# Summing over the head dimension: accumulating DMAs in place of indicator matmuls, with weight loads in 1 KB rows by contraction half

## The chip, the cores and the metric

The kernel runs on one core of one Trainium2 chip. The metric is the device time of one execution in microseconds (us); lower is better. A "span" is the profiled execution as the trace shows it; it is 1.5 to 2 us shorter than the time that is measured around it. Engines are called PE (matmuls), DVE (vector), ACT (activation), POOL (GpSimd, here it mainly issues DMAs) and SP (issues the loads).

## The reference

A gate mixes two branches over 2048 positions of width 512 (bfloat16):

```python
g = sigmoid((x * gate_w).sum(-1))               # one number a position
a = A(x)                                        # 32 heads of 16, each query sees 8 keys, 2 apart
b = B(x)                                        # layernorm, then an MLP over the POSITIONS
return g * a + (1 - g) * b

# A: logits[h, s, w] = sum_d q[h, s, d] * k[h, s - 2w, d] / 4 ; masked softmax over w (8) ; weighted sum of v ; @ wo
# B: u = gelu(h^T @ w1 + b1)  (2048 -> 1792) ; y = u @ w2 + b2  (1792 -> 2048) ; transposed back
```

The sum over `d` (16 head dimensions) is what this study is about. The layout splits the 16 dimensions 4 by 4: along one factor they lie in four tiles (`dl`), along the other in four neighbouring partitions. So DVE multiplies and adds over `dl`, and something must add partitions 4j, 4j+1, 4j+2 and 4j+3. The kernel's DVE operations all work within a partition and do not do that.

## The kernel before

The kernel is one list of operations with data dependences. A small planner in the file gives each a guessed duration, simulates the engines, and so fixes the order on every engine **before** the kernel runs. On the chip each engine works through its fixed order and waits at each operation for semaphores. An operation that is late holds everything behind it on its engine.

The parts that matter, with cuts:

```python
# the planner's guess of a DMA's end: one shared "DMA is free at" clock, 300 GB/s, 2 us of latency
def schedule(self, dma_bw=300e3, dma_lat=2.0, n_iter=3): ...
    xs = max(st + 0.3, dma_free); xd = max(op.nbytes / dma_bw, 0.05)
    dma_free = xs + xd
    op.end = max(dma_free, clock[e]) + dma_lat

# the sum over 4 neighbouring partitions: RP is a 0/1 matrix, 4 column groups at once, 16 matmuls a head half h
def f_sum(h, b0, with_gate): ...
    for wp in range(4):
        for c in range(4):
            ins = e.matmul(ps[32*c:32*c+32, 4+wp, :], lhsT=RP, rhs=sub(PB[b0], ...), tile_position=(0, 32*c))
A("pe", f_sum(h, b0, h == 0), ..., writes=LGB, name="sum%d" % h)
A("act", act(LOG[h], ps[:, 4:8, :], AF.Copy), 1.9, reads=LGB, writes=["log%d" % h], name="lev%d" % h)
# then on DVE: mask add, max tree (mx4, mx2, mx1), subtract (msub); on ACT exp; on DVE sum tree and normalisation (nrm)

# the normalised weights are copied to all partitions, a quarter of the positions each (four broadcasts, 512 KB each)
for c in range(4):
    prev = sch.dma("pool", ... dma_start(AVW[h] part c, ATT[h][32c:32c+32] repeated 4 times) ..., name="av%d_%d" % (h, c))

# weights times values for unit u (256 positions); for u = 3, 4, 5 half of the adds are an accumulating DMA
AV(tt(pv, V5..., AVW[h]..., ALU.mult), 4.4, ..., name="avm%d" % u)
if u in (3, 4, 5):
    sch.dma("pool", ... dma_start(pw(0, 4), pw(4, 4), accum_op=ALU.add) ..., name="avd%d" % u)
# later: avb (pair sum), avc -> ot[u], which PE's Wo matmuls of tiles 2u and 2u+1 need

def ld_w1(j):   # 7 loads of 1 MB, 256 columns each: rows of 512 bytes; ld_w2(j) likewise, 8 loads
    load("w1_%d" % j, W1H[j], w1v[:, :, 256*j:256*j+256], ...)
late_dep[0] = [qkd[0, 1]]   # w1_1, w1_2, wo, ... wait for the second accumulating DMA of the first q*k products
```

## Time and profile before

The kernel before takes 165.37 us (median of 3 runs, 165.23 to 165.86).

| What | Value | View |
|---|---|---|
| span, granted PE clock | 163.9 us, 1.0 | page, cores |
| PE in the chain of waits | 95% | page, part 4 |
| DVE busy | 92%, its waits on DMA 0.3 us | page, part 1; waits |
| attention's last sum on DVE ends | 158.7 us | timeline of DVE |

These are two lines of the page of the kernel before: busy time, share of the span and number of instructions of PE (part 1), and the lines of the chain that ended last (part 4).

```profile
PE 159.3 (97%) x793; PEld 77.5 (47%) x808; DVE 150.7 (92%) x126; ACT 70.2 (43%) x100; POOL 12.0 (7%) x36
...
PE ps L858 29%; PE ps L885 29%; PE ps L649 23%; PE ps L894 8%; PE ps L588 3%; DMA arena<-in_A_x_dram 2%; PE ps L722 1%; ACT arena L453 1%; PE ps L567 1%; PE ps L717 1%; DVE arena L579 0%; PE ps L604 0%
```

The chain is nearly all matmuls: L858 is the first MLP product, L885 the second, L649 the projections, L894 the Wo product. L722 with 1% is the indicator sum.

The waits view of the kernel before (who waited for whom: us in total, times, longest):

```profile
ACT arena L453 <- PE ps L894: 37.7, 11, 6.6
...
DVE arena L450 <- DMA arena<-arena: 0.3, 1, 0.3
```

ACT waits for PE a great deal, which costs nothing. DVE waits for a DMA once, 0.3 us.

The timeline of DVE before (start, length of the group, what, and in brackets the idle time ahead of it), and the last line of that of PE:

```profile
32.42 38.90 DVE L450 TENSOR_TENSOR arena<-arena 128x4096 bf16<-128x4096 bf16 x24
...
71.72 63.81 DVE L450 TENSOR_TENSOR arena<-arena 128x16 f32<-128x16 f32 x34
135.86 22.84 DVE L450 TENSOR_TENSOR arena<-arena 128x2048 bf16<-128x2048 bf16 x14 [0.33 <-DMA arena<-arena]
161.29 0.41 DVE L934 TENSOR_SCALAR arena<-ps,arena 128x128 bf16<-128x128 f32 x1 [2.59 <-PE ps L894]
```

```profile
155.90 5.35 PE L894 MATMUL ps<-arena 128*128 128x512 bf16 x28
```

DVE has no gap worth the name between 32 and 158.7 us (135.86 + 22.84), and PE's last Wo matmuls run to 161 us. The last two tiles of them (14 and 15) need DVE's last sum. So both engines are full, and DVE has about 1 us of slack.

How long POOL's DMAs take before, from issue to landing: first the two accumulating 1 MB DMAs of the products, then the eight broadcasts.

```profile
DMA to landing us min/median/max: 8.0/9.0/10.0
```

```profile
DMA to landing us min/median/max: 7.3/11.7/15.3
```

### The profile page before, as it was taken

The numbers are of one execution on the slowest core, as the hardware profiler recorded it, in microseconds if no ns is written. First come the engines' busy times: TensorE is split into PE (matmuls) and PEld (weight loads), VectorE is DVE, ScalarE is ACT, GpSimd is POOL, SyncE is SP. The second block draws the span as 40 slices with busy tenths as digits, with TensorE's granted clock in tenths as the row PEclk, the third lists the DMA queues.
The fourth block names the chain that finished last, engine by engine and source line by source line (L and its number), as shares of the span: only waits on it lengthen the run. The fifth ranks groups of instructions, "written<-read, shape, count | busy, mean of one in ns | idle before, by whom it ended". The sixth has DMA issues, their size and how long they took to land.

```text
span 163.9 us, 1989 instructions
## 1 busy us (share of the span) xinstructions
PE 159.3 (97%) x793; PEld 77.5 (47%) x808; DVE 150.7 (92%) x126; ACT 70.2 (43%) x100; POOL 12.0 (7%) x36
## 2 busy tenths in 40 slices
PE   7999999999999999999999999999999999999993
PEld 3755555555544444444444344444444444444641
DVE  0589989999999999999999999999999999999971
ACT  3357677766672379753111258111121111111164
POOL 3000021020000000004000000002200222000000
DMA  4999969909499094999998974990998799991014
GB/s 153 288 233 253 254 128 291 199 11 188 91 304 308 1 247 120 256 290 290 298 263 233 270 203 142 298 232 10 283 254 192 185 204 201 211 222 38 32 58 135
DMA packets 44684, 32.24 MB, mean 197 GB/s; under 512 B 7940, under 2 KB 42244, under 8 KB 44676
## 3 DMA queue, kind: packets, MB, share of 16 engines
q1 hardware_dynamic: 41444, 22.06, 51.9%
q0 software_dynamic: 2512, 9.44, 27.2%
q10 hardware_dynamic: 720, 0.62, 1.1%
q8 instruction: 6, 0.10, 0.2%
q14 instruction: 2, 0.02, 0.0%
HBM read 18.88 MB, written 2.10 MB: 128 GB/s over the span
## 4 chain that ended last, share of the span: by engine, by line
PE 95%; DMA 2%; ACT 1%; issue 1%; DVE 0%
PE ps L858 29%; PE ps L885 29%; PE ps L649 23%; PE ps L894 8%; PE ps L588 3%; DMA arena<-in_A_x_dram 2%; PE ps L722 1%; ACT arena L453 1%; PE ps L567 1%; PE ps L717 1%; DVE arena L579 0%; PE ps L604 0%
## 5 line engine op out<-in xcount | busy, mean ns | idle before, releaser
L450 DVE TENSOR_TENSOR arena<-arena 128x4096 bf16<-128x4096 bf16 (+8 forms) x79 | 132.0, 1718 | 1.9 <-ACT arena L453 0.6
L885 PE MATMUL ps<-arena 128*128 128x512 bf16 (+2 forms) x234 | 50.0, 366 | 0.2
L858 PE MATMUL ps<-arena 128*128 128x512 bf16 x218 | 48.5, 379 | 0.3
L453 ACT ACTIVATE arena<-ps,arena 128x512 bf16<-128x512 f32 (+1 forms) x30 | 21.8, 731 | 60.7 <-PE ps L894 37.7
L453 ACT ACTIVATE arena<-ps 128x512 bf16<-128x512 f32 (+3 forms) x53 | 32.9, 629 | 18.3 <-PE ps L649 10.9
L649 PE MATMUL ps<-arena 128*128 128x512 bf16 x173 | 38.0, 379 | 0.2
L885 PEld LDWEIGHTS ps<-arena 128*128 128x128 bf16 x238 | 22.8, 98 | 25.9
L858 PEld LDWEIGHTS ps<-arena 128*128 128x128 bf16 x224 | 21.7, 98 | 26.8 <-issue 0.8
L649 PEld LDWEIGHTS ps<-arena 128*128 128x128 bf16 x176 | 19.9, 113 | 18.0
L894 PE MATMUL ps<-arena 128*128 128x512 bf16 (+2 forms) x67 | 15.6, 366 | 0.1
L453 ACT ACTIVATE arena<-arena 128x16 f32<-128x16 f32 (+5 forms) x10 | 6.7, 678 | 9.7 <-DVE arena L450 9.7
L692 DVE BATCH_NORM_STATS2 arena<-arena 128x6 f32<-128x512 bf16 x16 | 9.9, 679 | 0.5 <-DMA arena<-in_A_x_dram 0.5
L954 ACT ACT_TABLE_LOAD x7 | 9.0, 1283 | 2.8 <-issue 2.7
L894 PEld LDWEIGHTS ps<-arena 128*128 128x128 bf16 x68 | 6.5, 98 | 7.3
L790 POOL DMA_DIRECT2D arena<-arena x8 | 4.3, 556 | 75.2 <-DVE arena L450 75.2
L706 DVE TENSOR_SCALAR arena<-arena 128x512 bf16<-128x512 bf16 x16 | 5.3, 406 | 0.0
L579 DVE COPY arena<-ps 128x256 bf16<-128x256 bf16 x4 | 1.1, 291 | 4.4 <-PE ps L567 4.2
L827 POOL DMA_DIRECT2D arena<-arena x3 | 3.6, 1209 | 17.7 <-DVE arena L450 17.7
L747 POOL DMA_DIRECT2D arena<-arena x2 | 2.5, 1268 | 31.5 <-DVE arena L692 21.5
L588 PE MATMUL ps<-arena 128*128 128x256 bf16 (+1 forms) x27 | 4.4, 313 | 0.2
L588 PEld LDWEIGHTS ps<-arena 128*128 128x128 bf16 x28 | 3.1, 119 | 1.1 <-DVE arena L579 0.4
L551 PE MATMUL ps<-const-bfloat16-1.0 128*128 128x512 bf16 (+1 forms) x9 | 2.7, 483 | 0.8 <-PEq L1004 0.8
(30 smaller groups left out, 14.4 us busy)
## 6 DMA issues: line engine op xcount, KB each, us to landing
arena<-in_B_w_dram SPq DMA_DIRECT2D x7, 1024.0 KB, 6.5
arena<-in_B_w_dram SPq DMA_DIRECT2D x8, 896.0 KB, 9.9
arena<-arena POOLq DMA_DIRECT2D x5, 1024.0 KB, 10.0
arena<-arena POOLq DMA_DIRECT2D x8, 512.0 KB, 11.7
out_dram<-arena SPq DMA_DIRECT2D x15, 128.0 KB, 2.3
arena<-in_A_x_dram SPq DMA_DIRECT2D x3, 512.0 KB, 4.7
arena<-in_A_wqkv_dram SPq DMA_DIRECT2D x2, 256.0 KB, 4.3
arena<-in_A_wqkv_dram SPq DMA_DIRECT2D x1, 512.0 KB, 6.5
```

The costliest lines, as they stand in the source:

```text
L450: return lambda e: e.tensor_tensor(out=o_, in0=a_, in1=b_, op=op_)
L453: return lambda e: e.activation(out=o_, in_=i_, func=f_, **kw)
L588: ins = e.matmul(ps[:, dl, c0:c1], lhsT=sub(WQKV, dt * 3 * D + dl, [(4, 128)]), rhs=XT[:, dt, c0:c1], start=(dt == 0 and hb == 0), stop=(d ...
L649: ins = e.matmul(ps[:, bank, :], lhsT=sub(WQKV, dt * 3 * D + tn * D + dl, [(4, 128)]), rhs=XT[:, dt, sb * 512:(sb + 1) * 512], start=(dt = ...
L692: A("dve", (lambda t_: lambda e: e.bn_stats(out=ST6[:, t_, :], in_=X[:, t_, :]))(t), 0.67, reads=["x%d" % t], writes=["st%d" % t], name="s ...
L706: A("dve", (lambda t_: lambda e: e.tensor_scalar(out=X[:, t_, :], in0=X[:, t_, :], scalar1=col(RSTD, t_), scalar2=col(NMR, t_), op0=ALU.mu ...
L790: prev = sch.dma("pool", (lambda d_, s_: lambda e: e.dma_start(d_, s_))(dst, src), 524288, sch.dsem("av%d_%d" % (h, c)), issue=1.0, reads= ...
L827: sch.dma("pool", (lambda o_, i_: lambda e: e.dma_start(o_, i_, accum_op=ALU.add, max_dma_last_dim=4096))(pw(0, 4), pw(4, 4)), 1800000, sc ...
L858: ins = e.matmul(ps[:, bank, :], lhsT=W1H[ft // 2][:, st, 128 * (ft % 2):128 * (ft % 2) + 128], rhs=X[:, st, :], start=(st == 0), stop=(st ...
L885: ins = e.matmul(ps[:, bank, 0:c1 - c0], lhsT=W2S[i // 2][:, ft, 128 * (i % 2):128 * (i % 2) + 128], rhs=UT[:, ft, c0:c1], start=(ft == 0) ...
L894: ins = e.matmul(ps[:, bank, 0:c1 - c0], lhsT=OT[:, i // 2, dl, 128 * (i % 2):128 * (i % 2) + 128], rhs=WO[:, dl, c0:c1], start=False, sto ...
L954: e.preload_act_table_set(want)
```

## The change

The intent is to take 32 matmuls off PE and two evictions off ACT: the four partitions are added by DMAs instead. The weight loads, all but the first of W1, get rows of 1 KB instead of 512 bytes: each load then holds half of the contraction for 512 columns, so four PSUM tiles stay open at a time. Eight of the sixteen layernorm applications move from DVE to ACT. DVE finishes the products of the first half-block before those of the second, and the gate's matmuls stand by themselves (both left out below). The diff, cut to its core:

```diff
-        dma_free = 0.0
+        dma_free = {"pool": 0.0, "hw": 0.0}          # the planner: POOL's DMAs and the loads no longer share a clock
...
+            src = w1v[:, 8*((j-1)%2):8*((j-1)%2)+8, 256+512*((j-1)//2):768+512*((j-1)//2)] if j else w1v[:, :, 0:256]
...
         for t in range(NST):
+            if t >= NST - 8:
+                A("act", act(X[:, t, :], X[:, t, :], AF.Identity, scale=col(RSTD, t), bias=col(NMR, t)), 0.6, ...)
+                continue
...
-            A("pe", f_sum(h, b0, h == 0), ...)
-            A("act", act(LOG[h], ps[:, 4:8, :], AF.Copy), 1.9, reads=LGB, ...)
+            for s_ in range(2):                       # s_: half of the head half, 512 positions
+                for k_ in range(2):                   # fa: partition 4j+k += partition 4j+k+2   (256 KB, accumulate)
+                    fold("fa%d_%d%d" % (h, s_, k_), ..., True, 550000, ...)
+            for s_ in range(2):
+                for k_ in range(2):                   # fb: logits = partition 4j (128 KB, copy)
+                    for c in (2*s_, 2*s_+1):          # fc: logits += partition 4j+1 (128 KB, accumulate)
+                        fold("%s%d_%d" % ("fb" if k_ == 0 else "fc", h, c), ..., k_ == 1, 100000*(1+k_), ...)
...
+        # MLP 1: ft 0, 1, then three groups of four tiles, first contraction half of all four, then the second
+        # MLP 2: the same, four tiles a group; a fixed order for the tail
```

Each of the four half-blocks thus has a chain of three DMA steps: fold (fa), copy (fb), accumulate (fc). POOL waits for the landing of one before it issues the next. The Trainium skill (DMA: Bandwidth & Descriptors, "Two DMAs through the same engine are not ordered") asks for just that: a DMA that reads what an earlier one wrote must wait for its semaphore. So three landings in a row are the price of this way of adding.

More of the change, by code (lines that the diff above doesn't have):

```diff
@@ L202, in _pass @@
                 clock[e] = st + op.dur
-                xs = max(st + 0.3, dma_free)
+                ring = "pool" if e == "pool" else "hw"
+                xs = max(st + 0.3, dma_free[ring])
                 xd = max(op.nbytes / dma_bw, 0.05)
-                dma_free = xs + xd
-                op.end = max(dma_free, clock[e]) + dma_lat
+                dma_free[ring] = xs + xd
+                op.end = max(dma_free[ring], clock[e]) + dma_lat
             else:
@@ L363, in bass_gated_mix__sliding_local_dilated__mixer_token_mlp__prompt_kernel @@
         W1N = NST * 256
-        W1H = [view(n_, BF16, [(256, NST), (1, 256)], extra=k_ * W1N)
-               for n_, k_ in (("W1", 0), ("W1", 1), ("W1", 2), ("XT", 0), ("XT", 1), ("W1", 0), ("W1", 1))]
+        W1H = [view(n_, BF16, [(512, NST // 2), (1, 512)] if j_ else [(256, NST), (1, 256)], extra=k_ * W1N)
+               for j_, (n_, k_) in enumerate((("W1", 0), ("W1", 1), ("W1", 2), ("XT", 0), ("XT", 1), ("W1", 0), ("W1", 1)))]
         W1R = ["w1s0", "w1s1", "w1s2", "w1x0", "w1x1", "w1s0", "w1s1"]
         def w2view(name, extra=0):
-            return view(name, BF16, [(256, NFT), (1, 256)], extra=extra)
+            return view(name, BF16, [(512, NFT // 2), (1, 512)], extra=extra)
         XTALL = ["xt0_%d_%d" % (t, k_) for t in range(4) for k_ in range(2)] + ["xt1", "xt2", "xt3"]
@@ L536, in ld_w1 @@
         def ld_w1(j):
-            w1ld[j] = load("w1_%d" % j, W1H[j], w1v[:, :, 256 * j:256 * j + 256], S * 256 * 2, [W1R[j]] + (XTALL if j in (3, 4) else []), order=j < 3,
+            src = w1v[:, 8 * ((j - 1) % 2):8 * ((j - 1) % 2) + 8, 256 + 512 * ((j - 1) // 2):768 + 512 * ((j - 1) // 2)] if j else w1v[:, :, 0:256]
+            w1ld[j] = load("w1_%d" % j, W1H[j], src, S * 256 * 2, [W1R[j]] + (XTALL if j in (3, 4) else []), order=j < 3,
                            after=[w1ld[j - 1]] if j > 3 else [])
         def ld_w2(j):
-            w1ld[7 + j] = load("w2_%d" % j, W2S[j], w2v[:, :, 256 * j:256 * j + 256], F * 256 * 2, ["w2_%d" % j] + W2ALIAS[j], order=False,
+            w1ld[7 + j] = load("w2_%d" % j, W2S[j], w2v[:, 7 * (j % 2):7 * (j % 2) + 7, 512 * (j // 2):512 * (j // 2) + 512], F * 256 * 2, ["w2_%d" % j] + W2ALIAS[j], order=False,
                                after=[w1ld[6 + j]])
@@ L705, in bass_gated_mix__sliding_local_dilated__mixer_token_mlp__prompt_kernel @@
         for t in range(NST):
+            if t >= NST - 8:
+                A("act", act(X[:, t, :], X[:, t, :], AF.Identity, scale=col(RSTD, t), bias=col(NMR, t)), 0.6,
+                  reads=["rstd", "nmr", "st%d" % t], writes=["x%d" % t], name="ln%d" % t, prio=10)
+                continue
             A("dve", (lambda t_: lambda e: e.tensor_scalar(out=X[:, t_, :], in0=X[:, t_, :], scalar1=col(RSTD, t_), scalar2=col(NMR, t_),
@@ L708, in bass_gated_mix__sliding_local_dilated__mixer_token_mlp__prompt_kernel, with f_gate @@
               reads=["rstd", "nmr", "st%d" % t], writes=["x%d" % t], name="ln%d" % t, prio=-10)
-        def f_sum(h, b0, with_gate):
-            def fn(e):
-                ins = None
-                if with_gate:
-                    for dt in range(4):
-                        for c in range(4):
-                            ins = e.matmul(ps[32 * c:32 * c + 32, 3, :], lhsT=GWREP[:, dt, :],
-                                           rhs=sub(XT, dt * S + c * UT_, [(HS, 2), (1, UT_)]),
-                                           start=(dt == 0), stop=(dt == 3), tile_position=(0, 32 * c))
-                for wp in range(4):
-                    for c in range(4):
-                        ins = e.matmul(ps[32 * c:32 * c + 32, 4 + wp, :], lhsT=RP, rhs=sub(PB[b0], (c // 2) * 4096 + 2 * wp * 512 + (c % 2) * UT_, [(512, 2), (1, UT_)]),
-                                       start=True, stop=True, tile_position=(0, 32 * c))
-                return ins
-            return fn
-        LGB = ["b4", "b5", "b6", "b7"]
+        def f_gate(e):
+            ins = None
+            for dt in range(4):
+                for c in range(4):
+                    ins = e.matmul(ps[32 * c:32 * c + 32, 3, :], lhsT=GWREP[:, dt, :],
+                                   rhs=sub(XT, dt * S + c * UT_, [(HS, 2), (1, UT_)]),
+                                   start=(dt == 0), stop=(dt == 3), tile_position=(0, 32 * c))
+            return ins
+        A("pe", f_gate, 1.0, reads=XTALL + ["gwrep"], writes=["b3"], name="gate", prio=-100)
+        A("act", act(E32, ps[:, 3, :], AF.Relu, scale=-1.0, bias=ZMAX), 0.6, reads=["b3"], writes=["e32"], name="zclip")
+        A("act", act(EB, E32, AF.Exp, scale=-1.0, bias=ZMAX), 0.6, reads=["e32"], writes=["eb"], name="zexp", table=LOGEXP)
         PLAN = {0: (0, 1, 2), 1: (1, 2, 0)}
@@ L735, in qk @@
                 sb = 2 * h + s_
-                A("dve", tt(sub(PB[b_], s_ * 4096, [(512, NW), (1, 512)]), sub(QH[h], dl * HS + s_ * 512, [(0, NW), (1, 512)]),
-                            sub(KH[h], dl * KR + PAD + s_ * 512, [(-2, NW), (1, 512)]), ALU.mult), 2.25,
+                A("dve", tt(sub(PB[b_], s_ * 4096, [(NW * UT_, 2), (UT_, NW), (1, UT_)]), sub(QH[h], dl * HS + s_ * 512, [(UT_, 2), (0, NW), (1, UT_)]),
+                            sub(KH[h], dl * KR + PAD + s_ * 512, [(UT_, 2), (-2, NW), (1, UT_)]), ALU.mult), 2.25,
                   reads=["q%d_%d" % (dl, sb), "k%d_%d" % (dl, sb)] + (["k%d_%d" % (dl, sb - 1)] if s_ else ["khalo" if h else "kpad"]),
-                  writes=[PS[b_][s_]], name="qk%d_%d_%d" % (h, dl, s_))
+                  writes=[PS[b_][s_]], name="qk%d_%d_%d" % (h, dl, s_), prio=-4 * (1 - s_))
             def qadd(x_, y_, s_, h=h):
                 A("dve", tt(sub(PB[x_], s_ * 4096, [(1, 4096)]), sub(PB[x_], s_ * 4096, [(1, 4096)]), sub(PB[y_], s_ * 4096, [(1, 4096)]), ALU.add), 2.25,
-                  reads=[PS[y_][s_]], writes=[PS[x_][s_]], name="qa%d_%d%d_%d" % (h, x_, y_, s_))
+                  reads=[PS[y_][s_]], writes=[PS[x_][s_]], name="qa%d_%d%d_%d" % (h, x_, y_, s_), prio=-4 * (1 - s_))
             def qaddd(x_, y_, s_, h=h):
@@ L755, in bass_gated_mix__sliding_local_dilated__mixer_token_mlp__prompt_kernel @@
                 qk(2, bb[2], s_)
-            for s_ in range(2):
                 qk(3, bb[1], s_)
                 qadd(bb[2], bb[1], s_)
-            for s_ in range(2):
                 qadd(bb[0], bb[2], s_)
             b0 = bb[0]
-            A("pe", f_sum(h, b0, h == 0), 1.2 + (1.0 if h == 0 else 0), reads=PS[b0] + ["rp"] + ((XTALL + ["gwrep"]) if h == 0 else []),
-              writes=LGB + (["b3"] if h == 0 else []), name="sum%d" % h, prio=-100, delay=0.2)
-            if h == 0:
-                A("act", act(E32, ps[:, 3, :], AF.Relu, scale=-1.0, bias=ZMAX), 0.6, reads=["b3"], writes=["e32"], name="zclip")
-                A("act", act(EB, E32, AF.Exp, scale=-1.0, bias=ZMAX), 0.6, reads=["e32"], writes=["eb"], name="zexp", table=LOGEXP)
@@ L767, in bass_gated_mix__sliding_local_dilated__mixer_token_mlp__prompt_kernel, with par, fold @@
-            A("act", act(LOG[h], ps[:, 4:8, :], AF.Copy), 1.9, reads=LGB, writes=["log%d" % h], name="lev%d" % h, prio=-30)
+            pst = PB[b0].ap[0][0]
+            def par(ap_, p0, dims, offs):
+                return bass.AP(ap_.tensor, ap_.offset + p0 * pst + offs, [list(d) for d in dims])
+            def fold(name, o_, i_, acc, nb, reads, writes):
+                kw = dict(accum_op=ALU.add, max_dma_last_dim=4096) if acc else {}
+                sch.dma("pool", lambda e: e.dma_start(o_, i_, **kw), nb, sch.dsem(name), issue=1.1, reads=reads, writes=writes, name=name)
@@ new lines, in bass_gated_mix__sliding_local_dilated__mixer_token_mlp__prompt_kernel @@
+            for s_ in range(2):
+                for k_ in range(2):
+                    fold("fa%d_%d%d" % (h, s_, k_), par(PB[b0], k_, [(4 * pst, 32), (1, 4096)], s_ * 4096), par(PB[b0], k_ + 2, [(4 * pst, 32), (1, 4096)], s_ * 4096),
+                         True, 550000, [PS[b0][s_]], ["fa%d_%d%d" % (h, s_, k_)])
+            for s_ in range(2):
+                for k_ in range(2):
+                    for c in (2 * s_, 2 * s_ + 1):
+                        fold("%s%d_%d" % ("fb" if k_ == 0 else "fc", h, c), psub(LOG[h], 32 * c, 32, 0, [(1, NW * UT_)]), par(PB[b0], k_, [(4 * pst, 32), (1, NW * UT_)], c * NW * UT_),
+                             k_ == 1, 100000 * (1 + k_), [PS[b0][s_], "fa%d_%d%d" % (h, s_, k_)], ["log%d_%d" % (h, c)])
@@ L768, in bass_gated_mix__sliding_local_dilated__mixer_token_mlp__prompt_kernel @@
+            LGR = ["log%d_%d" % (h, c) for c in range(4)]
             if h == 0:
                 A("dve", tt(psub(LOG[0], 0, 32, 0, [(UT_, NW), (1, PAD)]), psub(LOG[0], 0, 32, 0, [(UT_, NW), (1, PAD)]), MASK, ALU.add), 0.2,
-                  reads=["mask"], writes=["log0"], name="msk", prio=-30)
+                  reads=["mask"], writes=["log0", "log0_0"], name="msk", prio=-30)
             TR = ["s4", "s2", "s1"]
-            A("dve", tt(M4, LOG[h][:, 0:4, :], LOG[h][:, 4:8, :], ALU.max), 0.65, reads=["log%d" % h], writes=["s4"], name="mx4_%d" % h, prio=-30)
+            A("dve", tt(M4, LOG[h][:, 0:4, :], LOG[h][:, 4:8, :], ALU.max), 0.65, reads=["log%d" % h] + LGR, writes=["s4"], name="mx4_%d" % h, prio=-30)
@@ L773, in bass_gated_mix__sliding_local_dilated__mixer_token_mlp__prompt_kernel @@
             A("dve", tt(M2, M4[:, 0:2, :], M4[:, 2:4, :], ALU.max), 0.4, reads=["s4"], writes=["s2"], name="mx2_%d" % h, prio=-30)
             A("dve", tt(M1, M2[:, 0, :], M2[:, 1, :], ALU.max), 0.25, reads=["s2"], writes=["s1"], name="mx1_%d" % h, prio=-30)
-            A("dve", tt(LOG[h], LOG[h], sub(M1, 0, [(0, NW), (1, UT_)]), ALU.subtract), 1.2, reads=["s1"], writes=["log%d" % h], name="msub%d" % h, prio=-30)
+            A("dve", tt(LOG[h], LOG[h], sub(M1, 0, [(0, NW), (1, UT_)]), ALU.subtract), 1.2, reads=["s1"], writes=["log%d" % h] + LGR, name="msub%d" % h, prio=-30)
@@ L857, in fn @@
                 for st in range(8 * half, 8 * half + 8):
-                    ins = e.matmul(ps[:, bank, :], lhsT=W1H[ft // 2][:, st, 128 * (ft % 2):128 * (ft % 2) + 128], rhs=X[:, st, :],
-                                   start=(st == 0), stop=(st == NST - 1))
-                return ins
-            return fn
-        MLPB = [1, 2, 0, 1, 2, 0, 3, 1, 2, 0, 3, 1, 2, 0]
-        for ft in range(NFT):
-            bank = MLPB[ft]
-            for half in range(2):
-                PE(f_ph2(ft, bank, half), 1.735, ["x%d" % t for t in range(8 * half, 8 * half + 8)] + [W1R[ft // 2]], ["b%d" % bank],
-                   "ph2_%d_%d" % (ft, half))
-            A("act", act(UT[:, ft, :], ps[:, bank, :], AF.Gelu_apprx_tanh, bias=col(B1C, ft)), 0.7,
-              reads=["b%d" % bank, "b1c"], writes=["ut%d" % ft] + (["wq0", "wq1", "wq2", "wq3", "wk0", "wk1", "wv"] if ft == 0 else []), name="gel%d" % ft, table=GELU)
-            if ft % 2 == 1 and ft // 2 + 5 <= 6:
-                ld_w1(ft // 2 + 5)
+                    w_ = W1H[0][:, st, 128 * ft:128 * ft + 128] if ft < 2 else W1H[1 + 2 * ((ft - 2) // 4) + half][:, st % 8, 128 * ((ft - 2) % 4):128 * ((ft - 2) % 4) + 128]
@@ new lines, in fn, with mlp1 @@
+                    ins = e.matmul(ps[:, bank, :], lhsT=w_, rhs=X[:, st, :], start=(st == 0), stop=(st == NST - 1))
+                return ins
+            return fn
+        def mlp1(ft, half):
+            bank = (4 + ft) if ft < 2 else (ft - 2) % 8
+            j = 0 if ft < 2 else 1 + 2 * ((ft - 2) // 4) + half
+            PE(f_ph2(ft, bank, half), 1.735, ["x%d" % t for t in range(8 * half, 8 * half + 8)] + [W1R[j]], ["b%d" % bank], "ph2_%d_%d" % (ft, half))
+            if half:
+                A("act", act(UT[:, ft, :], ps[:, bank, :], AF.Gelu_apprx_tanh, bias=col(B1C, ft)), 0.7,
+                  reads=["b%d" % bank, "b1c"], writes=["ut%d" % ft] + (["wq0", "wq1", "wq2", "wq3", "wk0", "wk1", "wv"] if ft == 0 else []), name="gel%d" % ft, table=GELU)
@@ L873, in bass_gated_mix__sliding_local_dilated__mixer_token_mlp__prompt_kernel @@
+        for ft in range(2):
+            for half in range(2):
+                mlp1(ft, half)
+        ld_w1(5)
+        for g_ in range(3):
+            for half in range(2):
+                for ft in range(2 + 4 * g_, 6 + 4 * g_):
+                    mlp1(ft, half)
+                if (g_, half) == (0, 0):
+                    ld_w1(6)
         for j in range(8):
             ld_w2(j)
-        LAG = 5
-        ring[0], ring[1] = 0, [3, 4, 5, 6, 7, 1, 2, 0]
-        banks = {}
+        BK = {i: (4, 5, 6, 7, 0, 1, 2, 3)[i % 8] for i in range(NST)}
@@ L884, in fn @@
                 for ft in range(7 * half, 7 * half + 7):
-                    ins = e.matmul(ps[:, bank, 0:c1 - c0], lhsT=W2S[i // 2][:, ft, 128 * (i % 2):128 * (i % 2) + 128], rhs=UT[:, ft, c0:c1],
+                    ins = e.matmul(ps[:, bank, 0:c1 - c0], lhsT=W2S[2 * (i // 4) + half][:, ft % 7, 128 * (i % 4):128 * (i % 4) + 128], rhs=UT[:, ft, c0:c1],
                                    start=(ft == 0), stop=False)
@@ L902, in finish_tile @@
         def finish_tile(i):
-            bank = banks[i]
+            bank = BK[i]
             PE(f_wo(i, bank, 0, D), 0.87, ["ot%d" % (i // 2), "wo"], ["b%d" % bank], "wo%d" % i)
@@ L908, in finish_tile, with mlp2 @@
                     reads=["outs%d" % (i % 4)], name="d_out%d" % i)
+        TAILORDER = ([("m", 12, 0), ("m", 13, 0), ("w", 8), ("m", 14, 0), ("m", 15, 0, 0), ("w", 9), ("m", 15, 0, 1), ("m", 12, 1), ("m", 13, 1), ("m", 14, 1),
+                     ("m", 15, 1, 0), ("m", 15, 1, 1)] + [("w", i) for i in range(10, 15)])
         L = NST - 1
-        for i in range(L):
-            banks[i] = bank_()
-        head = ((0, 0), (1, 0), (2, 0), (0, 1), (1, 1), (2, 1))
-        for i, half in head + tuple((i, half) for i in range(3, L) for half in range(2)):
-            bank = banks[i]
-            PE(f_ph3(i, bank, half), 1.52, ["ut%d" % ft for ft in range(7 * half, 7 * half + 7)] + ["w2_%d" % (i // 2)], ["b%d" % bank], "ph3_%d_%d" % (i, half))
-            if half == 1 and i >= LAG:
-                finish_tile(i - LAG)
-        lastb = [bank_(), bank_()]
-        CH = ((0, 384), (384, 512))
-        for hf, (c0, c1) in enumerate(CH):
-            for half in range(2):
-                PE(f_ph3(L, lastb[hf], half, c0, c1), 0.77, ["ut%d" % ft for ft in range(7 * half, 7 * half + 7)] + ["w2_%d" % (L // 2)], ["b%d" % lastb[hf]],
-                   "ph3_%d_%d" % (L, half))
-        for i in range(L - LAG, L):
-            finish_tile(i)
+        CH = ((0, 384), (384, 512))
+        lastb = [BK[L], BK[8]]
+        def mlp2(i, half, hf=None):
+            bank = BK[i] if hf is None else lastb[hf]
+            c0, c1 = (0, D) if hf is None else CH[hf]
+            PE(f_ph3(i, bank, half, c0, c1), 1.52 * (c1 - c0) / D, ["ut%d" % ft for ft in range(7 * half, 7 * half + 7)] + ["w2_%d" % (2 * (i // 4) + half)], ["b%d" % bank],
+               "ph3_%d_%d%s" % (i, half, "" if hf is None else "ab"[hf]))
+        for b_ in range(3):
+            for half in range(2):
+                for i in range(4 * b_, 4 * b_ + 4):
+                    mlp2(i, half)
+                    if half and b_:
+                        finish_tile(i - 4)
+        for st_ in TAILORDER:
+            if st_[0] == "w":
+                finish_tile(st_[1])
+            else:
+                mlp2(*st_[1:])
         for hf, (c0, c1) in enumerate(CH):
```

## The prediction

> What bounds the kernel now. The chain of waits is PE for 95% of a 163.9 us span; the granted clock is 1.0 and no view shows PE waiting for weights or banks. But VectorE (DVE) is nearly co-critical. Its timeline has no gap over 0.5 us between 21.8 us and its last attention sum (ends 158.7 us), and the last five Wo groups on PE, of which the last two need that sum, run from 156.1 to 160.4 us. So PE has no idle time and DVE about 1 us of slack: a gain needs both to get shorter.
>
> What the change removes. PE: 32 indicator matmuls, 2 x about 0.9 us in the chain = 1.8 us (the gate's 1.0 us stays, only earlier). ACT: two evictions of the sums, 1.88 us each. DVE: 8 of 16 layernorm applications, 0.33 us start to start, 2.6 us; ACT takes them (about 0.6 us each) in a stretch where it is 70% busy, which the seven banks absorb. Without new waits both chains end 2 to 2.6 us earlier, about 163.
>
> What it adds. For each of four half-blocks a chain of three dependent DMAs from POOL: fold (accumulate), copy, accumulate; each waits for the landing of the one before. An uncontended accumulating DMA before (1 MB, issued at 35.0 us) had its first packet 1.8 us after issue start, moved 256 packets of 4 KB at about 0.35 us on 16 engines, and took 8.0 us. Estimate from that for the quarter-size fold: 3.5 to 4 us, then 2.5 and 3: about 10 us for a half alone. The Trainium skill (DMA: Bandwidth & Descriptors, "Issuing engines are not separate DMA queues") says that DMAs of all issuers share the same 16 engines. The trace agrees: with weight loads queued, POOL DMAs began 3.8, 5.0 and 3.2 us after issue, when the loads' backlog had nearly drained.
>
> The chains meet such backlogs. First half: folds issue near 41 us, just when W1 and Wo (2.6 MB, about 8 us) are released. Its result lands at 54 to 57 us, but DVE's fixed order wants it (mask add) near 52: 2 to 5 us stall. The last half issues near 95 to 98 us, beside three W2 loads: 0 to 4 us before the second max. 1 KB rows shorten loads a little (46 ns per 1 KB against 27 to 34 ns per 512 B) but loads were never waited for.
>
> Bigger: the second softmax is normalised later in DVE's order, directly before three multiplies (avm3 to avm5). Before, its end was followed by 22.5 us of DVE work until the first POOL-added sum was used, which landed 22 us after (four broadcasts of 9 to 15 us queue in front). Now only about 14 us of work lie between: up to 8 us stall, first at the multiply that needs the first broadcast (8.9 us to landing), then at that sum. PE's fixed order needs that sum for the seventh Wo group (tile 6), with 22 us of PE work behind it, so PE idles too.
>
> Sum: 165.4 - 2.3 (removed) + 2 to 5 (fold waits) + about 4 to 6 (broadcast and sum waits not hidden) is about 170.5 us; range 164.5 to 176. Faster over 2%: 0.04; within: 0.30; slower: 0.66.
>
> Right if: DVE's waits name DMA arena<-arena at the mask, the maxima, the multiplies and the pair sums, 5 to 12 us in total; PE shows a gap of 3 us or more before a Wo group (tile 6) at 135 to 147 us; DMA leaves PE's share of the chain below 92%.
>
> Wrong if: POOL packets interleave with loads instead of waiting for their backlog (folds land within 10 us, so 163 to 166); broadcasts without a weight load beside them land in 4 us; or PE waits for W1/W2 halves.

## The result, and the profile after

The changed kernel takes 200.83 us (median of 4 runs, 200.42 to 201.31) against 165.3 us before on the same chip. Executions over 1.5% slower than the fastest of the same kernel are left out of the means. The ratio is 1.2145 (95% interval 1.2103 to 1.2187). Ratios in this document are the mean time of one kernel's fast runs over that of the other's of the same rounds, so they are not quite the ratio of the quoted medians.

The page of the changed kernel: PE's busy line, the rows of DVE and of the granted clock in 40 slices (tenths), and the chain that ended last by engine and by line.

```profile
PE 167.7 (84%) x776; PEld 78.5 (39%) x776; DVE 148.8 (75%) x118; ACT 67.1 (34%) x104; POOL 31.0 (16%) x60
...
DVE  1689999999407960199992699999991950799970
...
PEclk9999999999999999999969999975759985589999
...
DMA 47%; DVE 30%; PE 14%; issue 4%; POOL 2%; ACT 1%; SPq 0%; DVEq 0%; POOLq 0%
DMA arena<-arena 45%; DVE arena L451 25%; PE ps L903 7%; PE ps L912 4%; DVE arena L694 4%; DMA arena<-in_A_x_dram 2%; POOL arena L768 2%; PE ps L590 1%; DVE arena L712 1%; ACT arena L454 1%; PE ps L651 1%; SPq L495 0%; PE ps L569 0%; DVE arena L684 0%; DVE arena L701 0%
```

PE's share of the chain has gone from 95% to 14%. "DMA arena<-arena", DMAs from on-chip memory to on-chip memory, takes 45% of it. The row of DVE has holes (4, 0, 6, 2, 1, 5), and after 99 us PE's clock falls to 5 tenths in some slices.

The waits view after:

```profile
POOL arena L768 <- DMA arena<-arena: 40.9, 8, 7.4
DVE arena L451 <- DMA arena<-arena: 37.0, 5, 10.6
...
PE ps L912 <- DVE arena L451: 20.0, 2, 13.7
...
PE ps L903 <- ACT arena L454: 7.7, 2, 4.3
```

DVE's five large waits on DMA are 37.0 us, against 0.3 before. The span grew by 35.2 us (199.1 - 163.9). DVE's busy time fell by 1.9 us (150.7 to 148.8). So nearly the whole loss passes through these five waits. POOL itself waits 40.9 us inside the chains (L768 is the fold) for one step to land before it may issue the next.

Where the five are, from the timeline of DVE after (bracket: idle time ahead of the group, and what ended it):

```profile
60.93 0.20 DVE L451 TENSOR_TENSOR arena<-arena 32x112 bf16<-32x112 bf16 x1 [9.15 <-DMA arena<-arena]
...
83.83 22.07 DVE L451 TENSOR_TENSOR arena<-arena 128x1024 bf16<-128x1024 bf16 x16 [10.65 <-DMA arena<-arena]
111.09 38.37 DVE L451 TENSOR_TENSOR arena<-arena 128x8192 bf16<-128x8192 bf16 x23 [5.19 <-DMA arena<-arena]
153.52 8.76 DVE L451 TENSOR_TENSOR arena<-arena 128x8192 bf16<-128x8192 bf16 x2 [4.06 <-DMA arena<-arena]
170.20 22.85 DVE L451 TENSOR_TENSOR arena<-arena 128x2048 bf16<-128x2048 bf16 x14 [7.92 <-DMA arena<-arena]
```

The first is the mask add (9.15 us, first half of head half 0), the second the first max (10.65 us, second half). The third is the first weighted multiply, waiting for its broadcast (5.19 us). The fourth and fifth are the multiply that needs the first broadcast of head half 1, and the first pair sum that reads what an accumulating DMA made (4.06 and 7.92 us).

The chains themselves, from the timeline of POOL after (each line a group of issues; bracket: what POOL waited for):

```profile
40.82 1.77 POOL L768 DMA_DIRECT2D arena<-arena  x2 [8.19 <-DVE arena L451]
48.89 1.14 POOL L768 DMA_DIRECT2D arena<-arena  x2 [6.30 <-DMA arena<-arena]
57.21 3.59 POOL L768 DMA_DIRECT2D arena<-arena  x4 [7.18 <-DMA arena<-arena]
68.25 1.14 POOL L768 DMA_DIRECT2D arena<-arena  x2 [7.45 <-DMA arena<-arena]
76.34 1.74 POOL L768 DMA_DIRECT2D arena<-arena  x2 [6.94 <-DMA arena<-arena]
...
118.01 1.83 POOL L768 DMA_DIRECT2D arena<-arena  x2 [12.90 <-DVE arena L451]
121.68 1.15 POOL L768 DMA_DIRECT2D arena<-arena  x2 [1.84 <-DMA arena<-arena]
124.95 1.75 POOL L768 DMA_DIRECT2D arena<-arena  x2 [2.12 <-DMA arena<-arena]
```

At 40.82 us the first folds are issued, at 48.89 the copies, at 57.21 the accumulates **and** the folds of the second half, at 68.25 and 76.34 us that half's copies and accumulates. The last chain, of head half 1, starts at 118.01 us: its steps follow each other after 3.7 and 3.3 us, not after 8. The record of landings gives the lengths from the first issue to the last landing that DVE waited for:

| Chain | Issued | Landed | Length | Weight loads beside it |
|---|---|---|---|---|
| head half 0, first half | 40.8 us | 60.8 (mask), 66.3 (all) | 20.0, 25.4 us | three at its start, four more later |
| head half 0, second half | 58.3 us | 83.7 us | 25.4 us | five |
| head half 1, first half | 89.1 us | 109.5 us | 20.4 us | four |
| head half 1, second half | 118.0 us | 129.3 us | 11.3 us | none |

The packets of POOL's queue show the difference at the start. In the last chain the first packet of the fold moves 1.47 us after issue. In the first chain it moves 5.18 us after, in the second chain the copies and the accumulates start after 4.00 and 4.36 us. In those microseconds the loads' queue moves 280 to 360 GB/s on average, and the new POOL DMA nothing. The third chain shows both cases side by side. Its two folds are issued at 89.07 and 89.66 us, a weight load at 90.20 us. The first fold lands after 3.68 us. The second moves its first packet 5.9 us after issue and lands after 9.02 us.

Landing times after, of the folds (L768), the broadcasts (L802) and the three pair-sum DMAs (L839):

```profile
DMA to landing us min/median/max: 2.7/7.4/10.3
```

```profile
DMA to landing us min/median/max: 8.7/12.6/17.9
```

```profile
DMA to landing us min/median/max: 17.0/17.8/20.4
```

The broadcasts were 7.3 to 15.3 us before; now 8.7 to 17.9. PE shows what becomes of it. This is its timeline around the largest gap:

```profile
155.95 1.03 PE L912 MATMUL ps<-arena 128*128 128x512 bf16 x4
156.82 1.67 PE L903 MATMUL ps<-arena 128*128 128x512 bf16 x7
172.21 1.89 PE L912 MATMUL ps<-arena 128*128 128x512 bf16 x4 [13.72 <-DVE arena L451]
```

L912 at 172.21 us is the Wo group of tile 6. It waits 13.72 us for DVE's pair sum, with about 22 us of PE work behind it in the fixed order. (The other L912 wait, 6.24 us, is that of tile 2.) Those four matmuls take 1.89 us where others take 1.03. The Trainium skill (TensorE: Matmul & The Clock Gate, "Part 1: The HAM clock gate") says that PE's clock drops to half after about 3.4 us of idling. The trace agrees: PE has nothing to do from 158.5 us on, and the granted clock, 1.00 from 159 to 162 us, is 0.50 from 163 to 172 us (windows view).

### The profile page after: what moved, and what is told of

Same layout as the page of the kernel before. It is cut to its first block, busy times and chain, and to the rows that moved or that the text cites. A ratio compares the mean times of both kernels' runs of the same rounds, so it can differ in the third digit from the quotient of the medians.

```text
span 199.1 us, 1964 instructions
## 1 busy us (share of the span) xinstructions
PE 167.7 (84%) x776; PEld 78.5 (39%) x776; DVE 148.8 (75%) x118; ACT 67.1 (34%) x104; POOL 31.0 (16%) x60
## 4 chain that ended last, share of the span: by engine, by line
DMA 47%; DVE 30%; PE 14%; issue 4%; POOL 2%; ACT 1%; SPq 0%; DVEq 0%; POOLq 0%
DMA arena<-arena 45%; DVE arena L451 25%; PE ps L903 7%; PE ps L912 4%; DVE arena L694 4%; DMA arena<-in_A_x_dram 2%; POOL arena L768 2%; PE ps L590 1%; DVE arena L712 1%; ACT arena L454 1%; PE ps L651 1%; SPq L495 0%; PE ps L569 0%; DVE arena L684 0%; DVE arena L701 0%
## 5 line engine op out<-in xcount | busy, mean ns | idle before, releaser
L903 PE MATMUL ps<-arena 128*128 128x512 bf16 (+2 forms) x238 | 57.0, 401 | 7.7 <-ACT arena L454 7.7
L454 ACT ACTIVATE arena<-ps,arena 128x512 bf16<-128x512 f32 (+1 forms) x30 | 20.7, 735 | 57.9 <-PE ps L912 42.2
L903 PEld LDWEIGHTS ps<-arena 128*128 128x128 bf16 x238 | 24.4, 105 | 39.7 <-issue 9.6
L912 PE MATMUL ps<-arena 128*128 128x512 bf16 (+2 forms) x68 | 17.7, 402 | 20.0 <-DVE arena L451 20.0
L454 ACT ACTIVATE arena<-arena 128x512 bf16<-128x512 bf16 (+6 forms) x18 | 13.2, 733 | 58.5 <-DVE arena L451 58.4
L454 ACT ACTIVATE arena<-ps 128x512 bf16<-128x512 f32 (+2 forms) x51 | 28.9, 578 | 10.7 <-PE ps L651 6.3
L871 PEld LDWEIGHTS ps<-arena 128*128 128x128 bf16 x224 | 21.9, 98 | 26.4
L768 POOL DMA_DIRECT2D arena<-arena x24 | 18.8, 939 | 73.0 <-DMA arena<-arena 40.9
L651 PEld LDWEIGHTS ps<-arena 128*128 128x128 bf16 x176 | 19.8, 113 | 18.2 <-ACT arena L454 0.4
L912 PEld LDWEIGHTS ps<-arena 128*128 128x128 bf16 x68 | 6.7, 104 | 29.0 <-DVE arena L451 21.4
L802 POOL DMA_DIRECT2D arena<-arena x8 | 5.1, 899 | 18.2 <-DVE arena L451 18.1
L748 POOL DMA_DIRECT2D arena<-arena x2 | 2.5, 1270 | 27.9 <-DVE arena L694 19.9
L839 POOL DMA_DIRECT2D arena<-arena x3 | 3.6, 1215 | 13.0 <-DVE arena L451 13.0
L590 PEld LDWEIGHTS ps<-arena 128*128 128x128 bf16 x28 | 3.0, 117 | 1.1 <-DMA arena<-in_A_wqkv_dram 0.5
```

The source lines that it names most:

```text
L454: return lambda e: e.activation(out=o_, in_=i_, func=f_, **kw)
L590: ins = e.matmul(ps[:, dl, c0:c1], lhsT=sub(WQKV, dt * 3 * D + dl, [(4, 128)]), rhs=XT[:, dt, c0:c1], start=(dt == 0 and hb == 0), stop=(d ...
L651: ins = e.matmul(ps[:, bank, :], lhsT=sub(WQKV, dt * 3 * D + tn * D + dl, [(4, 128)]), rhs=XT[:, dt, sb * 512:(sb + 1) * 512], start=(dt = ...
L768: sch.dma("pool", lambda e: e.dma_start(o_, i_, **kw), nb, sch.dsem(name), issue=1.1, reads=reads, writes=writes, name=name)
L802: prev = sch.dma("pool", (lambda d_, s_: lambda e: e.dma_start(d_, s_))(dst, src), 524288, sch.dsem("av%d_%d" % (h, c)), issue=1.0, reads= ...
L839: sch.dma("pool", (lambda o_, i_: lambda e: e.dma_start(o_, i_, accum_op=ALU.add, max_dma_last_dim=4096))(pw(0, 4), pw(4, 4)), 1800000, sc ...
```

## The experiments

The theory after the result: the fold's results arrive too late for DVE's fixed order, because each of the three steps can pay anew for the loads that are queued beside it. Rivals: the other parts of the change; the mere traffic; a chain that is this long with or without loads; an order that is merely badly planned. All kernels gave correct results. Times are medians of the fast runs, ratios are to the kernel before in the same rounds.

### e1: the fold undone, all else kept

```diff
-            for s_ in range(2): ... fold(fa), fold(fb), fold(fc)
+            A("pe", f_sum(b0), 1.2, reads=PS[b0] + ["rp"], writes=LGB, name="sum%d" % h, prio=-100, delay=0.2)
+            A("act", act(LOG[h], ps[:, 4:8, :], AF.Copy), 1.9, reads=LGB, writes=["log%d" % h], ...)
-            bank = (4 + ft) if ft < 2 else (ft - 2) % 8
+            bank = (ft + 3) % 4                       # the sums need banks 4 to 7
```

> The changed kernel with only the fold undone: sum matmuls and their eviction return (MLP banks 0 to 3, since the sums take 4 to 7), all else of the change stays. Theory (the 37 us of DVE waits after the change are waits on the fold chain, and on the broadcasts that it pushes late): all of the loss goes, 162.5 to 166.5 us, DVE waits on DMA under 3 us. Rival (the 1 KB half loads, four open tiles, the tail order or the layernorms on ACT cost too): stays over 175 us.

Measured: 166.76 us, ratio 1.0091 (1.0065 to 1.0117), slightly above the expected range. The waits view of this run:

```profile
DVE arena L451 <- DMA arena<-arena: 1.8, 2, 1.1
...
PE ps L734 <- DVE arena L451: 1.2, 2, 0.8
```

34 of the 35.5 us are gone, and so are DVE's waits (1.8 us). The rest of the change is not the cause. It costs 1.4 us here, and PE waits 1.2 us for the products of the two sums (see e10).

### e2: the fold alone, on the kernel before

```diff
+ (the fold, its product layout, the gate matmul by itself and the planner's two DMA clocks, as in the change)
  (weight loads of 512-byte rows, tile order, layernorms on DVE: as before)
```

> The kernel before with only the fold added (with its planner's separate DMA ring and product layout); weight loads, tile order and layernorms as before. Theory: the fold alone makes nearly the whole loss, 190 to 206 us, with waits of DVE on DMA of 25 to 45 us. Rival: under 175 us.

Measured: 207.66 us in the three fast runs (a fourth, 210.78 us, was slow). Their mean is 1.256 times that of the kernel before in these rounds. DVE waits 40.5 us on DMA. The fold alone is worse than the whole change, by 7 us, and a little over the expected range. With the fold in place the rest of the change therefore helps. Which part of it does was not separated.

### e5: the fold as traffic only

The sums are on PE as in e1. All 24 fold DMAs run too, after the sums, but their results go to partitions that nobody reads.

```diff
+            sop = A("pe", f_sum(b0), ...)             # as in e1
+            fold(..., deps=[sop])                     # fb, fc write partitions 4j+2 of the product buffer, not the logits
```

> The kernel with the sums back on PE (166.8 us), plus all the fold DMAs as mere traffic: same number, sizes and three-step dependence, started after the sum matmuls; their results go to partitions that nobody reads, so no softmax waits for them. They do hold the product buffers until they end. Theory (the loss is waiting for the chain, not the bytes): 166 to 174 us, what is over 167 being waits for a product buffer or for later broadcasts, at most 8 us. Rival (the added traffic slows the other DMAs and engines by itself): over 185 us.

Measured: 173.06 us, ratio 1.0437 (1.04 to 1.0474). So the traffic and the held product buffers cost about 6 us over e1. The other 28 us, by difference, are the waiting for the results. The split is rough, since the chains start later here and the planned order is another. In this run DVE waits 7.6 us on DMA, the longest 3.4 us for a product buffer that the chain still held, and PE 4.8 us for a late sum.

### e4: the first loads out of the way, early

```diff
-        late_dep[0] = [qkd[0, 1]]
+        late_dep[0] = []                              # w1_1, w1_2 and wo are loaded from 23 us on
```

> The changed kernel, but the two W1 loads and Wo are released at once (about 21 us) instead of after the first-stage accumulating DMA at 39 us, so that no load is queued when the first folds are issued. Theory (a POOL DMA waits for the backlog of queued loads): the first two folds land in 3.5 to 5 us instead of 7.8 and 8.8, the mask's wait falls from 9.2 us to 2 to 6 us; the earlier accumulating DMAs get slower by 3 to 5 us instead; 192 to 199 us in total. Rival (the chain is long by itself, loads or not): folds still take 7 to 9 us and the mask's wait stays at 8 us or more.

Measured: 197.95 us, ratio 1.198 (1.192 to 1.2041). The total is in the expected range, but both expected steps were missed: the folds landed in 5.5 and 6.2 us instead of 3.5 to 5, and the mask's wait was 8.7 us instead of 2 to 6. The folds were faster than in the changed kernel (7.8 and 8.8 us), but not alone: the first-stage accumulating DMA had been delayed and was still in the queue (it landed at 48.1 us). The copies took 7.1 us and the accumulates 8.5 us beside the next W1 loads. The run does not tell the theories apart. What it shows is that clearing the first step alone did not help the mask: the later two steps again had loads beside them.

### e6: the second half's folds ahead of the first half's copies on POOL

```diff
-                        fold("%s%d_%d" % ("fb" if k_ == 0 else "fc", h, c), ...)
+                        fold(..., after=[fal] if h == 0 else [])      # fal: the last of the four folds
```

> The changed kernel, but on POOL, for the first head half, all four folds are issued before the copies and final accumulates. Theory (in-order POOL: the second half's folds, ready at 49.5 us, were issued only at 58.3 us because the queue stood at a wait for the first half's copies): the second pair is issued at 50 us, the second chain ends 6 to 10 us sooner (before 77 us instead of 83.7), and the wait at the first max falls from 10.7 us to under 4 us while the mask's wait may grow by 1 to 3 us; 192 to 198 us. Rival (the second chain is bound by DMA traffic alone): it still ends after 80 us and the total stays at 199 us or more.

Measured: 197.93 us in the three fast runs (a fourth, 202.98 us, was slow), ratio 1.1997 (1.1925 to 1.2069), at the upper end of the expected range. The second folds are issued at 50.5 us instead of 58.3, that chain ends at 74.3 us instead of 83.7, and the wait at the first max falls from 10.65 to 1.2 us. The mask's wait, which was expected to grow, falls to 6.7 us. So POOL's strict order had held the second chain back by 8 us. But the total falls by only 2.9 us, because DVE's waits as a whole hardly move:

```profile
DVE arena L451 <- DMA arena<-arena: 35.3, 6, 9.1
```

A wait of 6.9 us appears at the first max of head half 1, and that for the first broadcast grows from 5.2 to 6.9 us.

### e7: the loads held back until head half 0's chains have landed

The planned order is that of the changed kernel, apart from the gate's transpose, which goes ahead of the loads on SP. The loads themselves wait on the chip.

```diff
+                if op.name == "w1_1":                 # on SP; wo and all later loads stand behind it
+                    for n_ in ("fc0_0", "fc0_1", "fc0_2", "fc0_3"):
+                        e.wait_ge(fops[n_].dsem.handle, 16)
```

> The changed kernel in the same planned order, but the second and third W1 loads and Wo (and all loads behind them) wait until the first head half's whole fold chain has landed; the gate's transpose goes ahead of them. PE must then starve for W1 by 8 to 14 us near 55 us. Theory (queued loads double the chain, which by itself takes about 11 us as the last one in the trace did, 118.0 to 129.3): each of the first two chains takes 10 to 13 us instead of 20 and 25, the mask's wait falls from 9.2 to under 2.5 us and that of the first max from 10.7 to under 3 us; in spite of PE's gap the total falls to 180 to 194 us. Rival (the chain takes 20 us whatever else is queued): waits stay at 9 and 10 us or more and the total rises over 203 us.

Measured: 202.72 us, ratio 1.2245 (1.2218 to 1.2271). Everything that was said of the chains came true; the total did not. First POOL's timeline in this run, over the first two chains:

```profile
40.90 1.77 POOL L769 DMA_DIRECT2D arena<-arena  x2 [8.19 <-DVE arena L451]
44.48 1.14 POOL L769 DMA_DIRECT2D arena<-arena  x2 [1.80 <-DMA arena<-arena]
48.55 3.60 POOL L769 DMA_DIRECT2D arena<-arena  x4 [2.93 <-DMA arena<-arena]
54.70 1.14 POOL L769 DMA_DIRECT2D arena<-arena  x2 [2.55 <-DMA arena<-arena]
58.24 1.74 POOL L769 DMA_DIRECT2D arena<-arena  x2 [2.39 <-DMA arena<-arena]
```

The steps follow each other after 3.6 and 4.1 us (8 in the changed kernel). The first chain lands for the mask at 51.96 us, 11.1 us after its issue. The second, from 49.96 to 62.63 us, takes 12.7 us. The first packet of the folds moves 1.45 us after issue. DVE:

```profile
52.05 0.20 DVE L451 TENSOR_TENSOR arena<-arena 32x112 bf16<-32x112 bf16 x1 [0.19 <-DMA arena<-arena]
...
52.67 20.68 DVE L451 TENSOR_TENSOR arena<-arena 128x16 f32<-128x16 f32 x13
88.34 12.81 DVE L451 TENSOR_TENSOR arena<-arena 128x1024 f32<-128x1024 bf16 x9 [14.98 <-ACT arena L454]
```

The mask add waits 0.19 us instead of 9.15, and the first max not at all. Nothing but the queued loads was taken away (and the transpose moved ahead), so the loads are what doubled the chain. The same run has the counter-test: the chains of head half 1, which met the released loads, took 19.3 and 19.5 us. But 15 us of waiting come back at another place, for ACT. DVE's waits on DMA are still 22.5 us and those on ACT 15.6, together 38.1, so the total could not fall. PE and ACT show where the 15 us come from:

```profile
68.64 43.35 PE L872 MATMUL ps<-arena 128*128 128x512 bf16 x188 [13.54 <-DMA arena<-in_B_w_dram]
```

```profile
79.22 0.69 ACT L454 ACTIVATE arena<-ps,arena 128x512 bf16<-128x512 f32 x1 [23.39 <-PE ps L872]
...
84.39 0.69 ACT L454 ACTIVATE arena<-ps,arena 128x512 bf16<-128x512 f32 x1 [1.04 <-PE ps L872]
...
86.39 1.91 ACT L454 ACTIVATE arena<-arena 128x2048 bf16<-128x2048 bf16 x1
```

PE starves 13.5 us for W1, as it had to. ACT's fixed order has the GELUs of those starved tiles ahead of the exponential that DVE waits for (86.39 us). So the exponential comes late although its input was early. The expected total (180 to 194) overlooked that path.

### e8 and e9: the planner told the truth

```diff
-                op.end = max(dma_free[ring], clock[e]) + dma_lat
+                op.end = max(dma_free[ring], clock[e]) + (6.0 if ring == "pool" else dma_lat)
```

> The changed kernel, planned with 6 us instead of 2 us of completion latency for POOL's DMAs (near what the trace of the changed kernel shows), so DVE's fixed order puts the users of the folds and broadcasts later. The DMAs themselves are the same. Theory (part of the loss is the order, planned for folds of 3 to 5 us; the rest is that DVE has not enough independent work for four chains of 11 to 25 us): 182 to 196 us, DVE's waits on DMA fall from 37 to 20 to 30 us but do not vanish. Rival A (all of the loss is the order): under 170 us. Rival B (order does not matter, the chains bound it): 199 us or more.

Measured: 190.94 us in the three fast runs (a fourth, 193.96 us, was slow), ratio 1.1526 (1.1487 to 1.1564). The waits view:

```profile
PE ps L912 <- DVE arena L451: 24.7, 3, 22.0
...
DVE arena L451 <- DMA arena<-arena: 23.1, 5, 9.1
```

A better order is worth 9.9 us. DVE still waits 23.1 us on DMA, and PE 22.0 us in one piece for DVE. The reading of the rest is argued, not tested: DVE has 148.8 us of work in all and had about 1 us of slack before, so work that does not need the logits is too little to cover four chains of this length.

> The changed kernel with both repairs of order: the planner told the 6 us, and the four folds of the first head half issued before their copies. Theory (both only move waits; four chains, broadcasts and loads share one set of DMA engines): 186 to 192 us, DVE still waits 18 to 26 us on DMA, no better than 3 us under the true-latency run (191.1). Rival (the repairs add up and the fold becomes usable): under 180 us.

Both repairs together (e8's planner and e6's order): the three fast runs took 191.25, 193.28 and 193.67 us, ratio 1.1654 (1.1592 to 1.1717). That is slightly over the expected range and no better than e8 alone. The fourth, profiled run (196.82 us) was slow, so neither its time nor its trace is used here, and the expected waits stay unchecked. These two changes of order do not make the fold usable; other orders were not tried.

### e10: what is left of the rest of the change

```diff
-            A("pe", f_sum(b0), 1.2, ..., prio=-100, delay=0.2)      # as in e1
+            A("pe", f_sum(b0), 1.2, ..., prio=-100, delay=1.6)
```

> The kernel with the sums back on PE (166.8 us), with each sum placed one or two half tiles later in PE's fixed order. Theory (what is left of the rest of the change, 1.4 us over the kernel before, is PE waiting 0.8 and 0.4 us for the products of each sum): both waits vanish, 165.2 to 166.0 us, ratio to before 0.998 to 1.004: the rest of the change is worth nothing, because PE waited for no load before. Rival (half loads or tail order cost by themselves): stays at 166.5 us or more.

Measured over five rounds: 165.72 us, ratio 1.0023 (0.9989 to 1.0057). Two lines of its page:

```profile
PE 160.2 (98%) x808; PEld 77.2 (47%) x808; DVE 148.8 (91%) x118; ACT 74.4 (45%) x108; POOL 12.0 (7%) x36
...
PE 97%; ACT 1%; DVE 0%; issue 0%
```

PE is 97% of the chain again and the span is 163.9 us, that of the kernel before. Nearly all of the 1.4 us of e1 were thus PE's waits for two sums that stood too early in its order. Half loads, four open tiles, the tail order and the layernorms on ACT together gain nothing measurable. That fits the profile before, where PE waited for no weight load. No version beat the kernel before.

## Why the prediction was right or wrong

The direction and most of the places were right. The size was not: 170.5 us predicted, with 176 as the upper end, against 200.83. The step that failed is the length of the chains beside the loads, and so the waits of DVE that come of them: 5 to 12 us of waits in all were predicted, 37.0 us were measured.

- **What is removed.** "2 x about 0.9 us" on PE, the evictions and DVE's layernorms were read rightly, but did not matter once PE was no longer the chain. DVE's busy time fell by 1.9 us where 2.6 were expected.
- **The chain alone.** "about 10 us for a half alone" was right: 11.3 us without loads in the changed kernel, 11.1 and 12.7 us in e7.
- **Loads beside the chain: the term that was mis-sized.** "Its result lands at 54 to 57 us ... 2 to 5 us stall" let the first fold wait for the backlog once and the copy and the accumulate run free. But further loads are issued at 48.8, 58.2 and 58.6 us, so the later steps paid too. The first fold took 7.8 us and the first copy 7.8. Of the two accumulates one took 8.5 us; the one that the mask needed took 3.6 and ran free. It landed at 60.84 us instead of 54 to 57, and the mask waited 9.15 us. The second and third chains, also beside loads, took 25.4 and 20.4 us. e7 shows that it is the loads: without them the wait is 0.19 us.
- **A term that was missing.** The prediction named the first half and the last half, and gave no wait to the second half of head half 0 and to the broadcast behind it. These cost 10.65 and 5.19 us. POOL issued the second folds only at 58.3 us though they were ready at 49.5 us, since it stood at a wait for the first half's copies (e6 moves them to 50.5 us).
- **The last half.** "0 to 4 us before the second max" was right at its lower end, but by luck: no wait over 0.1 us is seen there. The prediction put this chain at 95 to 98 us beside three W2 loads. It came at 118 us, when DVE was so late that no load was left beside it. In e6 and e7, where loads were, the second max waited 6.9 and 7.9 us.
- **The broadcasts and pair sums behind the second softmax.** "up to 8 us" was of the right kind and too small: 4.06 + 7.92 = 12.0 us. The normalisation ended at 144.5 us and the pair sum started at 170.2, 25.7 us later, where about 22 had been taken from the run before. The DVE work between was 13.7 us (25.7 less the two waits), as predicted ("about 14"). Every run with the delayed softmax whose trace was used has this pair of waits, 3.8 to 4.5 and 7.1 to 9.2 us. With the softmax early again (e1) it is gone. It was not isolated by an experiment of its own.
- **PE's gap.** "3 us or more before a Wo group (tile 6) at 135 to 147 us" was the right group, not the right time: the gap was 13.72 us and ended at 172.2 us.
- **The sum.** "2 to 5" + "about 4 to 6" stood where 9.15 + 10.65 + 5.19 + 4.06 + 7.92 = 37.0 us were measured. The waits add up, since DVE has next to no slack in which to win one back.

Of the list of what would make it wrong, none came to pass as it was meant. Single folds did land within 7.8 to 10.3 us, but after a start that waited for the loads; only then did packets of both queues mix. Broadcasts did not land in 4 us, and PE did not wait for weights. What was wrong, the size of the waits, was not on the list.

## What to carry to other kernels

Work moved from a full engine to DMAs is not free because DMA is "another engine". Count dependent landings, multiply by the landing time with the traffic that will run beside them (here mostly 7 to 10 us a step, 2.7 to 4.3 in the chain that ran alone), and ask whether the consumer has that much other work: 1.8 us of PE time were exchanged for 37 us of DVE waits. Where the order is fixed ahead of time, a planner that prices a DMA at its best case can turn its delay into a stall (e8), and a faster chain bought by holding other loads back (e7) only moves the stall. Loads that nobody waited for were not worth making faster (e10).

## What the Trainium skill lacked or had wrong

- DMA: Bandwidth & Descriptors, "Anatomy of one DMA": its fit of about 2.0 us plus bytes / 436e3 gives an estimate of 2.3 us for the 128 KB copy and 2.6 us for the 256 KB fold. Alone the trace shows 2.73 to 2.79 and 3.38 to 4.30 us, so both are above it, the fold, an accumulate, by up to 1.7 us. With loads queued the same DMAs take 7.4 to 8.0 and 7.8 to 10.3 us. The page gives no figure for a POOL-issued DMA beside queued loads.
- DMA: Bandwidth & Descriptors, "Queues, rings and completion order": it says that each engine takes turns between queues packet by packet. In these traces POOL's DMA moves nothing for 4.0 to 5.2 us after issue while the loads' queue runs at 280 to 360 GB/s on average, against 1.45 to 1.47 us for a fold with no load queued. Only then do the two mix. Why the start waits is left open.
- DMA: Bandwidth & Descriptors, "Rules for kernel authors": an accumulating DMA is named as POOL's business, with no rate. Here, with no load beside it, a 4 KB packet of a fold took 0.33 us at the least (median 0.35 to 0.38) and one of a plain copy 0.16 us (median).
